# Side work placed by a list schedule at build time, seven products in another order, eight PSUM banks in rotation

## The chip, the core and the metric

One core of a Trainium2 chip runs the kernel in one launch. The metric is the device time of that launch in microseconds. A core has a matrix engine (PE, its weight loads shown apart as PEld), a vector engine (DVE), a scalar engine (ACT), a general engine (POOL) and an engine that issues most transfers (SP). Each takes its instructions strictly in the order in which the program wrote them; between engines, semaphores say when a result is there. Matmul results land in PSUM, which has eight banks; a bank can be written again only when its last reader is through.

## What is computed

A linear attention over 4 batches of 576 rows, a rank-32 mixing along the sequence, a dense two-layer block with 512 inputs and 2048 hidden features, and a mixture of 8 experts (512 to 1024 to 512) in which a gate chooses an expert for each row.

```python
u = x + h.transpose(0, 2, 1)                       # x: what attention gave, h: the rank-32 mixing
ch = np.maximum(u @ w_ch1, 0.0) @ w_ch2            # dense block, 2048 hidden
x = (u + ch)
...
for s in range(S):                                 # experts, batch by batch
    fresh_e = int(np.argmax(logits[b, s]))
    if s == 0 or local_gate[b, s] < 0.5:
        e = fresh_e
    else:
        e = prev_e if prev_e >= 0 else fresh_e
    ...
    h = np.maximum(x[b, s] @ w1[e], 0.0)
    out[b, s] = p[e] * (h @ w2[e])
```

## The kernel before

After the attention, all work is cut into 24 items. An item is one batch (576 columns, in two halves of 288) against one unit of 512 hidden features. Items 0 to 15 are the dense block: four units, each against four batches. Items 16 to 23 are the experts: for each batch the expert that most of its rows chose, in two units. (A loop at the end repairs the rows that chose another expert; it finds few or none.)

Numbers are float32, and a product of two is made of three matmuls on split values: each operand is kept as a high part in the matmul's type (`fp32r`) and the low remainder. So every operand needs an ACT cast (high part) and a subtraction on DVE or POOL (low part) before PE may use it. These casts and subtractions, the sums below, the conversion of the dense weights from 64-bit words (six DVE instructions and one POOL sum for each of eight pieces of a unit, `narrow`, L77 to L84) and the expert choice (`route`) are the side work.

The first layer of items 1 to 23 takes seven block products in place of eight (`seven_steps`), with sums of weight blocks (S1 to S4) and of input blocks (T1 to T4). A product is 12 matmuls of 288 columns. Results stay in PSUM in pairs of banks; DVE and ACT take them out, add them (`u2`, `u3`, `p1`, L799) and make the hidden features by `relu`: ACT writes `hhi` (L756), then DVE writes `hlo` (L757). Then come eight steps of the second layer (`mm2`, 12 matmuls each, L842 to L844), and DVE adds each result into `y` (L852). An item is so 84 + 96 = 180 matmuls in 15 steps; item 0 uses eight plain products (192 matmuls).

What sets the order: the program is written in one pass. After each step `side` moves three queues of generators on, `w` (next unit's weights), `x` (inputs of a coming item) and `r` (routing), a fixed number of yields each: one, or two in some items. Where a product needs an operand that isn't written yet, `need_w` or `need_x` runs its queue on until it is. PSUM for items comes from two pools, 3 banks and 2, chosen by a counter; three more banks belong to routing (`ps_r`). The routing of items 13 to 16 advances twice after every step, or once. `then(i)` names the inputs to be made for item i + 2. For i = 14 and for i = 15 that is the same key, expert input of batch 3, so these inputs are made twice.

Of the kernel before, what the change touches and what calls it, by code (L numbers as in the profile page):

```python
# [22 lines left out]
CH = 288  # L23
# [14 lines left out]
def model(ctx, tc, kq, vx, wphi, ident, up, vp, wff, wg, wmoe1, wmoe2, rconst, outT):  # L38
# [30 lines left out]
    def narrow(dst, raw, p, n, a=None):  # L69
# [7 lines left out]
        nc.vector.tensor_scalar(out=au, in0=hw, scalar1=0x7FFFFFFF, scalar2=None, op0=ALU.bitwise_and)  # L77
        nc.vector.tensor_scalar(out=b, in0=a, scalar1=F64_LO, scalar2=F64_MAX, op0=ALU.max, op1=ALU.min)
        nc.vector.tensor_scalar(out=au, in0=bu, scalar1=3, scalar2=0x3FFFFFFF, op0=ALU.logical_shift_left, op1=ALU.bitwise_and)
# [3 lines left out]
        nc.vector.tensor_scalar(out=bu, in0=au, scalar1=0xFF800000, scalar2=None, op0=ALU.bitwise_and)  # L83
        nc.vector.scalar_tensor_tensor(out=b, in0=lw, scalar=2.0 ** -52, in1=b, op0=ALU.mult, op1=ALU.mult)  # L84
        in_halves(nc.gpsimd, dst, a, b, n, ALU.add)
        rows.extend(own)
# [49 lines left out]
    tasks = {"w": [], "x": [], "r": []}  # L136

    def advance(kind):

        q = tasks[kind]  # L140
        if not q:
            return "none"
        said = next(q[0], "end")
        if said == "end":
            q.pop(0)
        return said

    def take(free):

        while not free:  # L150
            yield "blocked"
        return free.pop(0)
# [6 lines left out]
    def raw_dma():  # L159

        while order and rawfree:
# [7 lines left out]
            raws.append(t)  # L169

    def fetch():

        raw_dma()
        t = raws.pop(0)
        f = yield from take(rows)
        if wff.dtype == F32:
            nc.gpsimd.tensor_copy(out=f[:, :512], in_=t.bitcast(F32)[:, :512])
        else:
            yield from narrow(f[:, :512], t, 128, 512, f[:, :512])
        rawfree.append(t)  # L180
        raw_dma()
        return f
# [8 lines left out]
    def w_end(u, s, f, eng, back=None, apart=True):  # L191

        w = u.w[s] = yield from take(wfree)
        nc.scalar.copy(out=w[:, 0], in_=f[:, :512])  # L194
        if apart:
# [5 lines left out]
        yield  # L201

    def w_first():

        for s in BLOCKS + VS:
            f = yield from fetch()
            yield
            yield from w_end(units[0], s, f, nc.gpsimd, rows, False)

    def w_sums():  # L210
# [4 lines left out]
        def whole(name, eng):  # L215
            f = yield from take(rows)
            both(eng, f, f32(u.w[name][:, 0]), f32(u.w[name][:, 1]), ALU.add)
            return f
# [6 lines left out]
        yield  # L225
        both(p, s3, a11, a21, ALU.subtract)
        yield
        both(v, a21, a21, a22, ALU.add)
        both(v, a11, a21, a11, ALU.subtract)
        rows.append(a22)  # L230
        yield
        yield from w_end(u, "S2", a11, v)
        yield from w_end(u, "S1", a21, p, rows)
        a12 = yield from whole("A12", v)
        both(v, a12, a12, a11, ALU.subtract)
        rows.append(a11)
        yield
        yield from w_end(u, "S3", s3, p, rows)
        yield from w_end(u, "S4", a12, p, rows)

    def w_seven(u, get, free, eng, p):
# [4 lines left out]
        both(p, s3, a11, a21, ALU.subtract)  # L246
        yield
        yield from w_end(u, "S3", s3, eng, rows)
        a22 = yield from get("A22")
        both(p, a21, a21, a22, ALU.add)  # L250
        yield
        yield from w_end(u, "A22", a22, eng, free)
        yield from w_end(u, "A11", a11, eng)
        both(p, a11, a21, a11, ALU.subtract)
        yield
        yield from w_end(u, "S1", a21, eng, free)
        a12 = yield from get("A12")
        yield from w_end(u, "A12", a12, eng)
        both(p, a12, a12, a11, ALU.subtract)
        yield  # L260
        yield from w_end(u, "S2", a11, eng, free)
        yield from w_end(u, "S4", a12, eng, free)

    def w_ffn(u):

        def get(name):
            f = yield from fetch()
            yield
            return f

        yield from w_seven(u, get, rows, nc.gpsimd, nc.gpsimd)
        for s in VS:
            f = yield from get(s)
            yield from w_end(u, s, f, nc.gpsimd, rows)

    halfraw = []

    def w_moe(u):

        if not halfraw:  # L280
# [6 lines left out]
        ahead_ = []  # L287

        def load():
            while halfraw and todo_:  # L290
# [6 lines left out]
                else:  # L297
                    nc.sync.dma_start(out=t, in_=wmoe2[e, 4 * u.g + int(name[1])].rearrange("o p f -> (o p) f"))
                ahead_.append(t)
# [8 lines left out]
        load()  # L308
        yield
        yield  # L310
        yield from w_seven(u, get, halfraw, nc.vector, nc.gpsimd)
        load()
        yield
        for s in VS:
            f = yield from get(s)
            yield from w_end(u, s, f, nc.vector, halfraw)

    def need_w(u, s):
        while s not in u.done:
            said = advance("w")  # L320
            assert said not in ("none", "blocked"), (u.kind, u.b, u.g, s, said)
# [3 lines left out]
    XS = ("B11", "T2", "B21", "T1", "T3", "T4", "B22")  # L325
    xo, xdone, xd = {}, set(), {}

    def x_end(key, s, r, eng):

        x = xo[key][s] = yield from take(xfree)  # L330
        nc.scalar.copy(out=x[:, 0], in_=r)  # L331
        yield
        for k in range(2):
            eng.tensor_tensor(out=x[:, 1, k], in0=r[:, k], in1=f32(x[:, 0, k]), op=ALU.subtract)  # L334
        xdone.add((key, s))
        yield
# [4 lines left out]
    def x_make(key, keep=True, plain=False, adds=nc.gpsimd, lows=nc.gpsimd):  # L341
# [7 lines left out]
        def add(a, c):  # L349
            r = yield from take(rows)  # L350
            x = as_x(r)
            for k in range(2):
                adds.tensor_tensor(out=x[:, k], in0=a[:, k], in1=c[:, k], op=ALU.subtract)  # L353
            yield
# [6 lines left out]
        def own(s):  # L361
            yield from x_end(key, s, part[s], lows)
            save(s, part[s])

        def made(s, r):
            if not plain:
                yield from x_end(key, s, as_x(r), lows)
            save(s, as_x(r))

        if plain:  # L370
            for s in ("B11", "B21", "B12", "B22"):
                yield from x_end(key, s, part[s], lows)
                if s != "B12":
                    save(s, part[s])
# [3 lines left out]
        t2 = yield from add(part["B22"], as_x(t1))  # L378
        yield from made("T2", t2)
        t4 = yield from add(as_x(t2), part["B21"])  # L380
        rows.append(t2)
        if not plain:
            yield from own("B21")
        yield from made("T1", t1)
        rows.append(t1)
        t3 = yield from add(part["B22"], part["B12"])
        yield from made("T3", t3)
        rows.append(t3)
        yield from made("T4", t4)
        rows.append(t4)  # L390
        if not plain:
            yield from own("B22")

    def x_load(key):

        xo[key] = {}
        got_ = []

        def load(m):
            r = yield from take(rows)  # L400
            nc.sync.dma_start(out=r, in_=xd[key][m])
            got_.append(r)

        for m in range(2):
            yield from load(m)
            yield
        for m, s in enumerate(XS):
            r = got_.pop(0)
            yield from x_end(key, s, as_x(r), nc.gpsimd)
            rows.append(r)  # L410
            if m + 2 < len(XS):
                yield from load(m + 2)

    def need_x(key, s):
        while (key, s) not in xdone:
            said = advance("x")
            assert said not in ("none", "blocked"), (key, s, said)
# [224 lines left out]
    def attn_step(S_):  # L642
# [41 lines left out]
        if S_ == 11:  # L684
            tasks["x"].append(x_make(("f", 0), plain=True))
        if S_ == 17:
            tasks["x"].append(x_make(("f", 1)))
# [25 lines left out]
    def fps():  # L713
        nps[0] += 1
        pool = late["psg"] if late and nps[0] % 5 < 2 else ps_f
# [23 lines left out]
    def then(i):  # L739

        if i < 3:
            return x_make(("f", 3), adds=nc.vector) if i == 1 else None
# [5 lines left out]
    def h_tiles(i, t, f):  # L748
# [3 lines left out]
        return hhi, hlo  # L752

    def relu(i, t, f, src):
        hhi, hlo = h_tiles(i, t, f)
        nc.scalar.activation(out=hhi, in_=src, func=ACTF.Relu)  # L756
        nc.vector.scalar_tensor_tensor(out=hlo, in0=src, scalar=0.0, in1=f32(hhi), op0=ALU.max, op1=ALU.subtract)  # L757

    def three(ps, w, x, j, first, stop):

        for k in range(2):
# [3 lines left out]
            nc.tensor.matmul(ps, lhsT=w[:, 1, c], rhs=x[:, 0, k], start=False, stop=(stop and k == 1), skip_group_check=True)  # L765

    def plain_steps(i):
# [3 lines left out]
        for t in range(2):  # L771
            for f in range(4):
                ps = fps()[:, :CH]
# [461 lines left out]
```

## Time and profile before

| | us |
|---|---|
| median of 3 runs | 918.18 (916.46 to 920.95) |
| the profiled execution | 914.94 |
| its span (first to last instruction) | 913.1 |
| PE busy | 810.7 (89%) |
| DVE busy | 650.9 (71%) |
| ACT busy | 351.8 (39%) |
| POOL busy | 422.6 (46%) |

The profiled execution is 1.84 us longer than its span. It has these stretches: attention, with item 0 in its last third (to about 200.9 us), items 1 to 12 (to 557.8), items 13 to 16 with the routing (to 703.8), items 17 to 22 (to 884), and item 23 with the end. Matmul durations overlap, since they are pipelined, so the distance from one start to the next tells the rate.

### The profile page before, as it was taken

To read this page: it belongs to the slowest core of one execution; us is meant where nothing else is said; L and a number is where in the kernel's file an instruction comes from. 1 tells how busy PE (TensorE), PEld (TensorE's weight loads), DVE (VectorE), ACT (ScalarE), POOL (GpSimd) and SP (SyncE) were. 2 spreads that over 40 slices of the span, in tenths; PEclk is the share of its full clock that TensorE was granted. 3 is DMA by queue.
4 is the path that set the end of the run, shared out by engine and by line. 5 is a ranking of instruction groups with operands and counts; after the bars stand their busy time and mean duration, and the time that the engine had idled before them with its cause. 6 is when DMAs were issued, how large, how long until landed. Compare 5 with 4: busy or idle time off the path is not lost. (4 is left out here: it accounts for less than half of the span.)

```text
span 913.1 us, 20785 instructions
## 1 busy us (share of the span) xinstructions
PE 810.7 (89%) x8368; PEld 768.6 (84%) x8368; DVE 650.9 (71%) x1300; ACT 351.8 (39%) x801; POOL 422.6 (46%) x522
## 2 busy tenths in 40 slices
PE   8999999997698879997899899879788879888897
PEld 6899988997697879987799798868688778887897
DVE  7899997458668865479654775688957866767654
ACT  5677776533221232121232231215224435345341
POOL 1123672147844595045870443536332764735712
PEclk9999999998899899999899899989899999998999
DMA  5443654012301341014320213032032143232411
GB/s 172 139 155 126 200 169 155 2 40 88 111 24 61 118 150 41 1 47 132 114 76 1 86 52 117 30 99 87 14 123 83 31 133 93 80 114 58 145 55 53
DMA packets 43618, 81.60 MB, mean 89 GB/s; under 512 B 4800, under 2 KB 21312, under 8 KB 43520
## 3 DMA queue, kind: packets, MB, share of 16 engines
q1 hardware_dynamic: 39808, 76.65, 26.6%
q10 hardware_dynamic: 3456, 3.46, 1.1%
q8 instruction: 66, 1.08, 0.5%
q14 instruction: 32, 0.26, 0.1%
q0 software_dynamic: 256, 0.15, 0.1%
HBM read 62.40 MB, written 17.84 MB: 88 GB/s over the span
## 5 line engine op out<-in xcount | busy, mean ns | idle before, releaser
L763 PE MATMUL psf<-x,w 128*128 128x288 f32 x676 | 214.2, 317 | 61.8 <-DVE hlo L757 30.4
L842 PE MATMUL psf<-hhi,w 128*128 128x288 f32 x768 | 235.9, 307 | 16.8 <-DVE u L799 10.5
L844 PE MATMUL psf<-hlo,w 128*128 128x288 f32 x768 | 233.5, 304 | 1.6 <-DVE hlo L757 1.3
L843 PE MATMUL psf<-hhi,w 128*128 128x288 f32 x768 | 231.6, 302 | 0.0
L764 PE MATMUL psf<-x,w 128*128 128x288 f32 x676 | 209.0, 309 | 0.0
L765 PE MATMUL psf<-x,w 128*128 128x288 f32 x676 | 208.2, 308 | 0.0
L763 PEld LDWEIGHTS psf<-x,w 128*128 128x128 f32 x676 | 135.8, 201 | 72.7 <-DVE hlo L757 33.4
L842 PEld LDWEIGHTS psf<-hhi,w 128*128 128x128 f32 x768 | 149.4, 194 | 23.0 <-DVE u L799 12.4
L334 POOL TENSOR_TENSOR x<-row,x 128x288 fp32r<-128x288 f32 x148 | 129.5, 901 | 80.0 <-ACT x L331 61.6
L844 PEld LDWEIGHTS psf<-hlo,w 128*128 128x128 f32 x768 | 149.4, 195 | 6.7 <-DVE hlo L757 6.3
L843 PEld LDWEIGHTS psf<-hhi,w 128*128 128x128 f32 x768 | 149.4, 195 | 0.0
L765 PEld LDWEIGHTS psf<-x,w 128*128 128x128 f32 x676 | 136.4, 202 | 0.2 <-DVE w L189 0.2
L764 PEld LDWEIGHTS psf<-x,w 128*128 128x128 f32 x676 | 136.1, 201 | 0.0
L67 POOL TENSOR_TENSOR row<-row,row 128x256 f32<-128x256 f32 x90 | 69.2, 790 | 98.4 <-DVE row L84 95.4
L67 POOL TENSOR_TENSOR w<-row,w 128x256 fp32r<-128x256 f32 x88 | 72.6, 848 | 79.7 <-ACT w L194 78.3
L852 DVE TENSOR_TENSOR y<-psf,y 128x288 f32<-128x288 f32 x160 | 69.1, 450 | 54.7 <-PE psf L844 54.3
L194 ACT CAST w<-row 128x512 fp32r<-128x512 f32 x53 | 32.7, 620 | 163.0 <-POOL row L67 154.5
L756 ACT ACTIVATE hhi<-u 128x288 fp32r<-128x288 f32 x92 | 38.6, 442 | 130.6 <-DVE u L799 130.6
L189 DVE TENSOR_TENSOR w<-raw,w 128x512 fp32r<-128x512 f32 x80 | 61.8, 778 | 32.3 <-ACT w L194 31.5
L799 DVE TENSOR_TENSOR u<-psf,p 128x288 f32<-128x288 f32 x92 | 40.8, 453 | 55.9 <-PE psf L765 44.5
L757 DVE SCALAR_TENSOR_TENSOR hlo<-u,hhi 128x288 fp32r<-128x288 f32 x92 | 55.0, 618 | 29.4 <-ACT hhi L756 29.4
L334 POOL TENSOR_TENSOR x<-y,x 128x288 fp32r<-128x288 f32 x56 | 49.0, 896 | 54.5 <-ACT x L331 29.6
(125 smaller groups left out, 1274.4 us busy)
## 6 DMA issues: line engine op xcount, KB each, us to landing
raw<-in_wff SPq DMA_DIRECT2D x32, 512.0 KB, 3.5
raw<-in_wmoe SPq DMA_DIRECT2D x64, 256.0 KB, 2.8
row<-xd SPq DMA_DIRECT2D x42, 288.0 KB, 3.5
kq<-in_kq SPq DMA_DIRECT2D x14, 576.0 KB, 4.8
vt<-in_vx SPq DMA_DIRECT2D x16, 325.0 KB, 3.1
xd<-row SPq DMA_DIRECT2D x16, 288.0 KB, 3.6
ys<-y SPq DMA_DIRECT2D x4, 1152.0 KB, 5.6
xd<-y SPq DMA_DIRECT2D x12, 288.0 KB, 4.3
```

Of the source, the lines that this page charges most:

```text
L67: eng.tensor_tensor(out=dst[:, sl], in0=a[:, sl], in1=b[:, sl], op=op)
L189: eng.tensor_tensor(out=out, in0=a, in1=b, op=op)
L334: eng.tensor_tensor(out=x[:, 1, k], in0=r[:, k], in1=f32(x[:, 0, k]), op=ALU.subtract)
L757: nc.vector.scalar_tensor_tensor(out=hlo, in0=src, scalar=0.0, in1=f32(hhi), op0=ALU.max, op1=ALU.subtract)
L763: nc.tensor.matmul(ps, lhsT=w[:, 0, c], rhs=x[:, 0, k], start=(first and k == 0), stop=False, skip_group_check=True)
L764: nc.tensor.matmul(ps, lhsT=w[:, 0, c], rhs=x[:, 1, k], start=False, stop=False, skip_group_check=True)
L765: nc.tensor.matmul(ps, lhsT=w[:, 1, c], rhs=x[:, 0, k], start=False, stop=(stop and k == 1), skip_group_check=True)
L799: nc.vector.tensor_tensor(out=out, in0=a, in1=c, op=op)
L842: nc.tensor.matmul(ps, lhsT=wh, rhs=hhi, start=(f == 0), stop=False)
L843: nc.tensor.matmul(ps, lhsT=wl, rhs=hhi, start=False, stop=False)
L844: nc.tensor.matmul(ps, lhsT=wh, rhs=hlo, start=False, stop=(f == 3))
L852: nc.vector.tensor_tensor(out=dst, in0=ps, in1=dst, op=ALU.add)
```

## The change

Routines that yielded at fixed places now yield in front of each instruction, at a `gate`. The builder keeps a clock for each engine (`free`) and for each tile (`touched`), moved by a cost formula per instruction and by 0.1325 for each matmul. In the stage after attention, a side instruction is written only if its engine would be through with it by PE's clock plus an allowance from a table (`SLACK`, by engine and step of the item). `pump` offers the gate to all side routines after every step; a routine that is needed at once runs with the gate forced open (`until`).

The products' order is now A11, S2, S1, S3, A22, A12, S4 (before: A11, S2, A12, S1, S3, A22, S4), so that of the inputs is B11, T2, T1, T3, T4, B21, B22. `mm2` sums features in the order 2, 3, 0, 1. The last two `relu` of an item stand behind the first `mm2` step. The second PSUM pool has 5 banks, routing's own pool is gone, and items and routing take the eight banks in turn. Routing advances twice after each of the last eight steps of an item alone. From i = 15 on, `then` names the inputs of item i + 3. The copy of `y` for the repair loop goes out in four transfers of a quarter. The operations and the engines that do them are otherwise the same.

```diff
+    SYNC = 0.15
+    SLACK = {"DVE": (1.5, 0.4, 1.5, 0.1, -0.2, -0.2, -0.2, 1.0, 1.0, 1.0, 0.3, 2.0, 2.0, 2.0, 1.5),
...
+    def cost(eng, n):
+        return {"DVE": 0.075 + n / 960, "ACT": 0.17 + n / 1330, "POOL": 0.05 + n / 365}[eng]
...
+    def book(eng, dur, *keys):
+
+        at = max([free[eng]] + [touched.get(id(k), 0.0) for k in keys])
+        free[eng] = at + dur
+        for k in keys:
+            touched[id(k)] = free[eng] + SYNC
+        return free[eng]
+
+    def gate(eng, dur, *keys):
+
+        if not late:
+            yield "step"
+        while late and not force[0]:
+            at = max([free[eng]] + [touched.get(id(k), 0.0) for k in keys])
+            if at + (0.0 if eng == "POOL" else dur) <= free["PE"] + SLACK[eng][at_step[0]]:
+                break
+            yield "wait"
+        emitted[0] += 1
+        if late:
+            book(eng, dur, *keys)
...
-    XS = ("B11", "T2", "B21", "T1", "T3", "T4", "B22")
+    XS = ("B11", "T2", "T1", "T3", "T4", "B21", "B22")
...
-        pool = late["psg"] if late and nps[0] % 5 < 2 else ps_f
+        pool = late["psg"] if late and nps[0] % 8 < 5 else ps_f
...
-        if i + 2 < n and not held(i):
-            key = x_key(i + 2)
-            return x_make(key, keep=False, adds=nc.vector) if key[0] == "m" else x_load(key)
+        to = i + 2 if i < 15 else i + 3
+        if to < n and not held(i):
+            key = x_key(to)
+            return x_make(key, to, keep=False, adds=nc.vector) if key[0] == "m" else x_load(key, to)
...
-        product("A12", "B21", pa, False, True)
-        for j in range(2):
-            relu(i, 0, j, pa[j])
-        yield
-        product("S1", "T1", pe, True, True)
+        product("S1", "T1", "e", True)
...
+        product("A12", "B21", "a", False)
...
+        late["rest"] = lambda: [relu(1, j, u2[j], t2[j]) for j in range(2)]
...
-        for f in range(4):
+        for k, f in enumerate((2, 3, 0, 1)):
...
-            advance("r")
+        if step >= steps - 8:
+            for _ in range(2):
+                advance("r")
...
-        for _ in range(2 if u.kind == "moe" or i % 4 in (0, 3) else 1):
-            if advance("w") == "blocked":
-                break
-        for _ in range(2 if i < 3 or i > 14 else 1):
-            if advance("x") == "blocked":
-                break
+        pump()
...
-    late["psg"] = ctx.enter_context(tc.tile_pool(name="ps_g", bufs=2, space=PSUM))
-    late["psr"] = ctx.enter_context(tc.tile_pool(name="ps_r", bufs=1, space=PSUM))
+    late["psg"] = ctx.enter_context(tc.tile_pool(name="ps_g", bufs=5, space=PSUM))
```

What this does to the order, at two places. First DVE in item 8, the stretch from the second to the fifth product; `row<-raw` and `row<-row` are weight conversion, `u`, `p` and `hlo` take results out of PSUM. Before:

```order
L83 TENSOR_SCALAR row_85<-row_91 128x512
L84 SCALAR_TENSOR_TENSOR row_85<-raw_92,row_85 128x512
L77 TENSOR_SCALAR row_87<-raw_93 128x512
L78 TENSOR_SCALAR row_90<-row_87 128x512
L79 TENSOR_SCALAR row_87<-row_90 128x512
L757 SCALAR_TENSOR_TENSOR hlo<-psf,hhi 128x288 x2
L81 SCALAR_TENSOR_TENSOR row_87<-raw_93,row_87 128x512
L83 TENSOR_SCALAR row_90<-row_87 128x512
L84 SCALAR_TENSOR_TENSOR row_90<-raw_93,row_90 128x512
L799 TENSOR_TENSOR u_3647<-psf,p_3643 128x288
```

The same engine and stretch of the changed kernel (L885 is the add, L887 `hlo`):

```order
L90 SCALAR_TENSOR_TENSOR row_87<-raw_92,row_87 128x512
L77 TENSOR_SCALAR row_85<-raw_93 128x512
L885 TENSOR_TENSOR u_3644<-psf,p_3640 128x288
L885 TENSOR_TENSOR p_3640<-psf,u_3644 128x288
L885 TENSOR_TENSOR u_3645<-psf,p_3641 128x288
L885 TENSOR_TENSOR p_3641<-psf,u_3645 128x288
L885 TENSOR_TENSOR u_3644<-u_3644,psf 128x288
L887 SCALAR_TENSOR_TENSOR hlo<-u_3644,hhi 128x288
L885 TENSOR_TENSOR u_3645<-u_3645,psf 128x288
L887 SCALAR_TENSOR_TENSOR hlo<-u_3645,hhi 128x288
L887 SCALAR_TENSOR_TENSOR hlo<-psf,hhi 128x288 x2
```

Conversion instructions stood in front of `hlo` in blocks of three to five; now none stands between the fourth product's add and the last `hlo` of the seven products, and the rest of the conversion follows one or a few at a time between the `y` adds. Second, DVE in item 15, where the routing's second half runs (`trps` is PSUM with transposed gate values, `r_cnt` counts votes). Before, in the products' part:

```order
L940 COPY row_86<-trps 8x320
L943 SCALAR_TENSOR_TENSOR row_90<-row_87,row_90 8x576
L945 TENSOR_REDUCE r_cnt<-row_90 8x1
L946 TENSOR_TENSOR row_86<-row_86,row_90 8x576
L189 TENSOR_TENSOR w_97<-raw_93,w_97 128x512
L799 TENSOR_TENSOR u_3647<-psf,p_3643 128x288
L799 TENSOR_TENSOR p_3643<-psf,u_3647 128x288
```

In the changed kernel, in the `mm2` part of the same item:

```order
L885 TENSOR_TENSOR y<-psf,y 128x288
L1114 COPY row_85<-psf 8x256
L1114 COPY row_90<-psf 8x256
L1114 COPY row_84<-psf 8x256
L1114 COPY row_85<-psf 8x320
L1114 COPY row_90<-psf 8x320
L1114 COPY row_84<-psf 8x320
L1117 SCALAR_TENSOR_TENSOR row_85<-row_90,row_85 8x576
L1119 TENSOR_REDUCE r_cnt<-row_85 8x1
L1120 TENSOR_TENSOR row_84<-row_84,row_85 8x576
L469 TENSOR_TENSOR row_91<-y 128x288
L885 TENSOR_TENSOR y<-psf,y 128x288
```

The routing left the products' part of the item, and all of it now stands between the `y` adds of eight steps.

## Rows read from the trace of the kernel before

**Rows 1.** Waits of PE, whole run: line, releaser: us, times, longest.

```profile
PE psf L763 <- DVE hlo L757: 30.4, 13, 6.2
PE psf L763 <- ACT p L804: 11.5, 6, 4.7
PE psf L763 <- DVE u L799: 10.7, 7, 3.4
PE psf L842 <- DVE u L799: 10.5, 7, 2.3
PE trps L936 <- DVE tr L925: 9.5, 4, 3.1
PE psf L763 <- DVE y L852: 6.9, 7, 1.8
PE psf L842 <- ACT hhi L756: 6.0, 13, 0.6
...
PE psf L763 <- ACT w L194: 2.1, 3, 1.0
PE psf L844 <- DVE hlo L757: 1.3, 4, 0.4
```

**Rows 2.** Stretches: length, busy PE, PEld, DVE, ACT, POOL, clock, DMA.

```profile
200.90:557.80 356.90, 316.27 (x2162) 305.89 (x2161) 243.09 (x476) 94.59 (x205) 195.32 (x240) 0.93 0.23 73
557.80:703.80 146.00, 120.44 (x831) 112.65 (x830) 111.76 (x282) 43.08 (x94) 53.87 (x66) 0.92 0.25 81
703.80:884.00 180.20, 156.71 (x1082) 149.29 (x1082) 126.43 (x225) 80.20 (x172) 101.28 (x114) 0.97 0.32 94
```

**Rows 3.** Stretches again, of single items: 1, 6 and 15.

```profile
200.94:235.20 34.26, 28.78 (x183) 27.19 (x181) 31.44 (x58) 11.35 (x24) 24.24 (x28) 0.90 0.30 96
363.13:387.03 23.90, 23.90 (x182) 23.90 (x181) 10.99 (x26) 4.58 (x11) 1.57 (x2) 1.00 0.01 1
628.57:667.20 38.63, 30.48 (x210) 28.40 (x208) 33.61 (x80) 13.12 (x27) 21.37 (x26) 0.91 0.16 53
```

**Rows 4.** Timeline of DVE in item 8: start, length, line.

```profile
424.29 0.76 DVE L78 TENSOR_SCALAR row<-row 128x512 f32<-128x512 f32 x1
425.08 0.83 DVE L79 TENSOR_SCALAR row<-row 128x512 uint32<-128x512 uint32 x1
425.83 0.81 DVE L757 SCALAR_TENSOR_TENSOR hlo<-psf,hhi 128x288 fp32r<-128x288 f32 x2
```

**Rows 5.** Timeline of PE in item 8, the start after those rows.

```profile
426.33 0.40 PE L763 MATMUL psf<-x,w 128*128 128x288 f32 x1 [3.25 <-DVE hlo L757]
```

**Rows 6.** Timeline of PE, matmuls after a wait and later.

```profile
309.31 0.44 PE L765 MATMUL psf<-x,w 128*128 128x288 f32 x1
...
314.73 0.29 PE L765 MATMUL psf<-x,w 128*128 128x288 f32 x1
```

**Rows 7.** Groups by shape, DVE, items 1 to 12: dearest and cheapest conversion line.

```profile
L81 DVE SCALAR_TENSOR_TENSOR row<-raw,row 128x512 uint32<-128x512 uint32 x24 | 19.6, 815 | 0.3
...
L83 DVE TENSOR_SCALAR row<-row 128x512 uint32<-128x512 uint32 x24 | 12.0, 500 | 0.4
```

**Rows 8.** Groups by shape, DVE, items 13 to 16: sums of inputs.

```profile
L353 DVE TENSOR_TENSOR row<-y 128x288 f32<-128x288 f32 x8 | 4.4, 593 | 0.0
...
L353 DVE TENSOR_TENSOR row<-row,y 128x288 f32<-128x288 f32 x4 | 3.4, 879 | 0.0
...
L353 DVE TENSOR_TENSOR row<-y,row 128x288 f32<-128x288 f32 x4 | 1.6, 438 | 0.0
```

**Rows 9.** Groups by shape, DVE, `hlo` from `u`: items 1 to 12.

```profile
L757 DVE SCALAR_TENSOR_TENSOR hlo<-u,hhi 128x288 fp32r<-128x288 f32 x48 | 30.6, 657 | 18.1 <-ACT hhi L756 18.1
```

**Rows 10.** The same group in item 6 alone (364.5 to 386).

```profile
L757 DVE SCALAR_TENSOR_TENSOR hlo<-u,hhi 128x288 fp32r<-128x288 f32 x4 | 1.7, 456 | 1.0 <-ACT hhi L756 1.0
```

**Rows 11.** The same group in item 1 alone (201 to 235).

```profile
L757 DVE SCALAR_TENSOR_TENSOR hlo<-u,hhi 128x288 fp32r<-128x288 f32 x4 | 3.6, 908 | 2.1 <-ACT hhi L756 2.1
```

**Rows 12.** The page's costliest groups: low parts of weights on DVE.

```profile
L189 DVE TENSOR_TENSOR w<-raw,w 128x512 fp32r<-128x512 f32 x80 | 61.8, 778 | 32.3 <-ACT w L194 31.5
```

More of the change, by code (lines that the diff above doesn't have):

```diff
@@ L135, in model @@
     ereg = {}
-    tasks = {"w": [], "x": [], "r": []}
-    def advance(kind):
[L140 to L150, printed above, removed]
+    free = {"PE": 0.0, "DVE": 0.0, "ACT": 0.0, "POOL": 0.0}
+    touched = {}
+    threads = []
+    force = [False]
+    emitted = [0]
+    SYNC = 0.15
+    SLACK = {"DVE": (1.5, 0.4, 1.5, 0.1, -0.2, -0.2, -0.2, 1.0, 1.0, 1.0, 0.3, 2.0, 2.0, 2.0, 1.5),
+             "ACT": (0.3, 1.0, 1.0, 1.0, 0.5, 0.0, 0.5, 1.0, 1.0, 1.0, 1.0, 1.0, 1.0, 1.0, 1.0),
+             "POOL": (2.0,) * 15}
@@ L168, in raw_dma, with fetch @@
                 nc.sync.dma_start(out=t, in_=wff[u.g, i].bitcast(U32))
[L169 to L182, printed above, removed]
+            touched[id(t)] = max(free["PE"], touched.get(id(t), 0.0)) + 4.0
+            raws.append((u, name, t))
+    pieces = {}
+    def fetch(u):
+        for name in ("A21", "A11", "A22", "A12") + VS:
+            raw_dma()
+            while not raws or raws[0][:2] != (u, name) or len(rows) < 2 or len(rows) < 5 and not force[0]:
+                yield "blocked"
+                raw_dma()
+            t, f = raws.pop(0)[2], rows.pop(0)
+            if wff.dtype == F32:
+                yield from gate("POOL", cost("POOL", 512), t, f)
+                nc.gpsimd.tensor_copy(out=f[:, :512], in_=t.bitcast(F32)[:, :512])
+            else:
+                while not rows:
+                    yield "blocked"
+                parts = narrow(f[:, :512], t, 128, 512, f[:, :512], True)
+                for n_ in range(6):
+                    yield from gate("DVE", cost("DVE", 512), t, f)
+                    next(parts, None)
+                if late:
+                    book("POOL", cost("POOL", 512), f)
+            rawfree.append(t)
+            raw_dma()
+            pieces[u, name] = f
     def both(eng, out, a, b, op):
@@ L361, in own @@
         def own(s):
[L362 to L371, printed above, removed]
+            if late:
+                spawn("x", due, x_end(key, s, part[s], lows, None, lambda: save(s, part[s])))
+            else:
                 yield from x_end(key, s, part[s], lows)
@@ L374, in x_make, with made, then @@
                     save(s, part[s])
+        def made(s, r, last_=True):
+            def then():
+                save(s, as_x(r))
+                if keep:
+                    touched[id(r)] = max(free["PE"], touched.get(id(r), 0.0)) + 3.0
+                if last_:
+                    rows.append(r)
+            if plain:
+                then()
+            elif late:
+                spawn("x", due, x_end(key, s, as_x(r), lows, r, then))
+            else:
+                yield from x_end(key, s, as_x(r), lows)
+                then()
+        if plain:
+            for s in ("B11", "B21", "B12", "B22"):
+                yield from own(s)
         else:
```

434 lines of the change are left out of this document (274 added, 160 removed).

## The prediction

> **What bounds the kernel now.** I read the stretches first, because the stages differ. In items 1 to 12, 13 to 16 and 17 to 22 PE is the busiest engine, but it is neither always busy nor always at full clock: granted 0.93, 0.92 and 0.97 [rows 2]. Single items show what it can do. Item 6, which has almost no side work, takes 23.90 us with PE busy throughout and clock 1.00 [rows 3]: that is the floor of an item. Items 1 and 15 take 34.26 and 38.63 us, with DVE busy 31.44 and 33.61 [rows 3]. So side work comes in lumps, and DVE is the engine that is late in the lumps. On average it isn't the bound: over items 1 to 12 DVE is busy 243.1 us, and twelve floors are 12 x 23.90 = 286.8 [rows 2, 3].
>
> The list of PE's waits says what for [rows 1]. Four rows are L763, the first matmul of a product, released by whoever last read a bank (`hlo`, `p`, `u`, `y`): 30.4 + 11.5 + 10.7 + 6.9 = 59.5 us. These are waits for a free bank. Three rows are L842 and L844, second-layer matmuls that wait for hidden features: 10.5 + 6.0 + 1.3 = 17.8. The routing's transposes wait 9.5, weights 2.1. Together 88.9 us. One of them is seen whole in item 8: DVE does two conversion instructions of 0.76 and 0.83 us, then `hlo` twice, and PE starts the next product after 3.25 us without work [rows 4, 5].
>
> A second loss hangs on these. After a wait a matmul lasts 0.44 us, later 0.29 [rows 6]; the granted clock is then at the lower of its two levels, 1.2 in place of 2.4 GHz. What that costs is PE's busy time over the floor: 316.3 - 286.8 = 29.5 in items 1 to 12; 156.7 - 6 x 23.90 = 13.3 in items 17 to 22; in items 13 to 16, 120.4 us hold 831 matmuls, of which 831 - 4 x 180 = 111 or so are the routing's, at the stage's mean (120.4 / 831) 16.1 us, so 120.4 - 95.6 - 16.1 = 8.7 [rows 2, 3]. Sum 51.5. In all 140 of 914.9 us can be had at most.
>
> **The change part by part.**
>
> *Eight banks.* With five banks a new product waits for a reader a few steps back; an item takes 16 banks, so with eight a bank comes round after about eight steps, some 12 us at floor rate (23.90 x 8 / 15). None of the four L763 kinds reaches back so far, and the 59.5 us go. What is late next: the first `mm2` step takes the bank of A11 and A12, whose last reader is the `hlo` of A12, now the sixth product of seven. Only S4 (12 matmuls, 23.90 x 12 / 180 = 1.6 us) lies between. The nearest row for such a short chain is L842 waiting for `hhi`, 6.0 us in 13, 0.46 each [rows 1]. I charge 0.46 to each of 23 items: 10.6. Bounds: nothing, or all 59.5, if DVE is as late as now.
>
> *Products' order, features in the order 2, 3, 0, 1, last relu behind the first `mm2` step.* Each gives DVE a product or a step more before PE asks. Against the 17.8 us I take half, 8.9 left; bounds 0 and 17.8.
>
> *The list schedule.* It removes no conversion. Eight pieces of six instructions stand in each of three units, 144 instructions at 0.50 to 0.82 us, so 72 to 117 us of DVE in items 1 to 12 [rows 7]. What changes is their place: item 8 loses its blocks in front of `hlo`, and items that had none get some. By the order, weight-conversion instructions in items 2 to 11 are now about 6 to 18 an item; before it was 24 or none. At 18 x 0.82 + 11 = 26 us of DVE for the worst, against 31.4 in item 1 now, the fullest item is still a little over the floor, the others under it. This is the cover for the bank term: without it DVE stays late, and the half case below holds.
>
> *Routing.* The chain on DVE is the same, and PE's transposes still wait for it. It is now squeezed into eight steps of an item instead of fifteen, beside eight `y` adds. I charge the 9.5 us one and a half times, 14.3; bounds 0 and 19.
>
> *The second making of batch 3's inputs goes.* It takes eight of 16 sums on DVE, (4.4 + 3.4 + 1.6) / 2 = 4.7 us [rows 8], with seven casts and 14 subtractions on ACT and POOL. In items 13 to 16 DVE has 111.8 us of 146.0 [rows 2], so it is on the path for part of this at most. I count 0 beside the waits; bounds 0 and 4.7.
>
> *Queues.* Four transfers of `y` in place of one add SP instructions and no wait on the path; in-order neighbours are input loads for two items later. The gate's yields also cut the input making during attention finer, but PE is nearly always busy there. Both 0, bounds 2 either way.
>
> *Sum.* Waits left: 10.6 + 8.9 + 14.3 + 2.1 = 35.9 of 88.9, a gain of 53.0. The low clock follows the waits: 51.5 x 35.9 / 88.9 = 20.8 stay, gain 30.7. Together 83.7: 914.94 - 83.7 = 831.2. The median of the runs lies 918.18 - 914.94 = 3.2 over the profiled execution, so I say 835.
>
> **A rule against it.** `hlo` made from `u` takes 456 ns in item 6, where POOL is busy 1.57 of 23.90 us, and 908 ns in item 1, where POOL is busy 24.24 of 34.26; the mean over items 1 to 12 is 657 [rows 3, 9 to 11]. The builder's formula prices it at 0.075 + 288 / 960 = 0.375 us wherever it stands. The Trainium skill, page "SBUF — State Buffer", section "Who interferes with whom", says that a vector instruction with two SBUF inputs contends with a GpSimd instruction that reads SBUF, and that the one that comes second is held for the whole of the other. By that rule the change does harm that the sum leaves out, since POOL's work is spread over all items and no item is left undisturbed. The trace agrees as far as rows 10 and 11 go. What it would give is the second rival.
>
> **The rivals.**
>
> 1. *DVE stays late* (0.18). The formula undercharges DVE and charges routing nothing, so the bank waits turn into waits for `hlo` and `u`, and only half of them go. For it: 0.50 to 0.82 us measured against 512 / 960 + 0.075 = 0.61 [rows 7]. Against it: 243 of 287 us leave room. Left 29.8 + 17.8 + 14.3 + 2.1 = 64.0; gain 24.9 + 51.5 x 0.28 = 39.3; 914.94 - 39.3 + 3.2 = 879.
>
> 2. *POOL slows DVE in every item* (0.13). Six `hlo` an item read two SBUF tiles; at 908 in place of 657 ns [rows 9, 11] that is 12 x 6 x 0.25 = 18 us on DVE in items 1 to 12. If all of it reaches PE: 853.
>
> 3. *Near the floor* (0.17). Only the routing's 9.5 and the weights' 2.1 stay: gain 77.3 + 51.5 x 77.3 / 88.9 = 122.1, so 796.
>
> 4. *Slower: a side instruction blocks DVE's queue* (0.06). DVE waits 31.5 us in front of L189 for a cast that follows a POOL sum that follows a transfer [rows 12]; today most of that lies where DVE is idle anyway. If the builder's clock thinks the operand there and puts L189 in front of an add, everything behind it on DVE waits, then PE. With no bank wait saved: 31.5 x (1 + 51.5 / 88.9) = 49.7 more, 968. It decides the sign once such new waits exceed the 53.0 saved.
>
> That the change doesn't do what it says is excluded for the place of the work by the order of both kernels.
>
> **How the numbers follow.** The forecast of 835 has 0.46 (815 to 850). Rivals 1, 2 and 3 are faster too, except the tail of rival 1, whose bounds reach no change. A measurement of this kernel tells 0.5%, 4.6 us, from none. Faster: 0.46 + 0.13 + 0.17 + 0.15 = 0.91; within: 0.03; slower: 0.06. For 8 in 10 the range goes from the floor case to a little past the half case: 797 to 892.
>
> **What would show it.** L763 rows released by `hlo`, `p`, `u` and `y` should fall from 59.5 to some 10 us, and what stays should stand at the first `mm2` step (L1009) or at S3, which adds into banks that the `u2` adds must have read. The transposes should keep 10 to 20 us. Items 2 to 12 should take 24 to 27 us each, all alike, clock 0.97 or more. The stretch of items 13 to 16 should stay the slowest, some 33 us an item. If DVE's idle time in front of L189 grows while adds are queued, rival 4 is at work; if `hlo` from `u` takes 0.8 us or more in every item, rival 2; if second-layer waits grow past 20 us, rival 1.

## The result, and the profile after

The changed kernel takes 824.76 us (median of 4 runs, 823.74 to 830.81), the kernel before 917.32 in the same comparison. The ratio is 0.8997, 95% interval 0.8954 to 0.9041: faster, by some 92 us where 83 were forecast, and 10 us under the predicted 835. The profiled execution is the slowest of the four: 830.81 us, span 829.0. The forecast for it was 831.2.

The three stretches of the profile after, items 1 to 12, 13 to 16 and 17 to 22 (length, busy time of each engine, granted clock, share of DMA, GB/s), answer to [rows 2]:

```profile
197.47:509.89 312.42, 297.36 (x2163) 293.34 (x2162) 256.51 (x474) 94.61 (x205) 206.72 (x240) 0.98 0.26 85
509.89:640.92 131.03, 112.69 (x831) 106.62 (x830) 105.55 (x275) 40.51 (x90) 52.55 (x66) 0.96 0.24 80
640.92:799.91 158.99, 150.01 (x1083) 149.07 (x1082) 121.20 (x223) 76.72 (x167) 90.26 (x100) 0.96 0.36 109
```

They are 44.5, 15.0 and 21.2 us shorter; the attention in front ends 3.4 us earlier. DVE's busy time in the first stretch has not fallen, it has grown by 13 us: the work is the same and only stands elsewhere.

Single items of after, 2, 9, 12 and 15, beside [rows 3]:

```profile
225.43:255.99 30.56, 26.95 (x183) 26.71 (x182) 28.06 (x50) 7.04 (x16) 23.39 (x27) 0.89 0.32 96
408.17:437.91 29.74, 26.18 (x182) 25.53 (x181) 25.56 (x40) 10.09 (x21) 24.21 (x31) 0.94 0.33 106
485.98:509.89 23.91, 23.91 (x183) 23.91 (x182) 12.07 (x26) 7.86 (x17) 11.38 (x14) 1.00 0.07 27
572.29:609.70 37.41, 30.15 (x209) 28.58 (x208) 34.34 (x91) 11.79 (x25) 15.14 (x18) 0.91 0.22 75
```

Item 12 is at the floor, as are items 7, 8, 11, 19 and 21. Items 2 and 9 are not, and item 15, with its routing, hardly moved.

What PE waits for in after, the whole run (us, times, longest), answers to [rows 1]:

```profile
PE psf L912 <- DVE u L885: 20.9, 9, 4.3
PE psf L1130 <- DVE r_cnt L1119: 8.3, 4, 2.5
PE psf L1110 <- DVE tr L1099: 5.6, 4, 2.5
PE psf L1011 <- DVE hlo L887: 4.1, 4, 3.1
PE psf L1009 <- ACT hhi L901: 2.0, 5, 0.4
PE psf L914 <- DVE w L279: 1.4, 1, 1.4
```

Together 42.3 us, of 88.9 before. The first row is one place: the nine matmuls that open S3, the fourth product, which adds into a bank that DVE must first have read to make `u`. One of them, in item 18, on DVE and PE (start, length, line, idle time before and its releaser):

```profile
672.96 0.99 DVE L279 TENSOR_TENSOR w<-raw,w 128x512 fp32r<-128x512 f32 x1 [1.56 <-ACT w L285]
673.87 0.81 DVE L885 TENSOR_TENSOR u<-psf,p 128x288 f32<-128x288 f32 x2
...
674.37 0.61 PE L912 MATMUL psf<-x,w 128*128 128x288 f32 x1 [4.33 <-DVE u L885]
```

DVE waits 1.56 us in a side instruction for a cast, with the two `u` adds behind it, and PE waits for those: rival 4's mechanism. It stands so in items 18, 20 and 22, 9.0 of the 20.9 us. In items 1, 2, 3, 5 and 15, 10.4 us, DVE runs side work without a pause right up to the two adds, which is what rival 1 described.

### The profile page after: what moved, and what is told of

Same layout as the page of the kernel before. It is cut to its first block, busy times and chain, and to the rows that moved or that the text cites. A ratio compares the mean times of both kernels' runs of the same rounds, so it can differ in the third digit from the quotient of the medians.

```text
span 829.0 us, 20784 instructions
## 1 busy us (share of the span) xinstructions
PE 776.8 (94%) x8368; PEld 749.7 (90%) x8368; DVE 653.4 (79%) x1292; ACT 345.8 (42%) x794; POOL 422.1 (51%) x508
## 5 line engine op out<-in xcount | busy, mean ns | idle before, releaser
L1009 PE MATMUL psf<-hhi,w 128*128 128x288 f32 x768 | 231.5, 301 | 2.0 <-ACT hhi L901 2.0
L1011 PE MATMUL psf<-hlo,w 128*128 128x288 f32 x768 | 229.0, 298 | 4.2 <-DVE hlo L887 4.1
L1010 PE MATMUL psf<-hhi,w 128*128 128x288 f32 x768 | 228.7, 298 | 0.0
L912 PE MATMUL psf<-x,w 128*128 128x288 f32 x676 | 205.0, 303 | 20.9 <-DVE u L885 20.9
L914 PE MATMUL psf<-x,w 128*128 128x288 f32 x676 | 204.4, 302 | 1.4 <-DVE w L279 1.4
L913 PE MATMUL psf<-x,w 128*128 128x288 f32 x676 | 204.4, 302 | 0.0
L447 POOL TENSOR_TENSOR x<-row,x 128x288 fp32r<-128x288 f32 x140 | 124.6, 915 | 93.9 <-ACT x L444 70.7
L912 PEld LDWEIGHTS psf<-x,w 128*128 128x128 f32 x676 | 132.2, 196 | 23.0 <-DVE u L885 23.0
L1009 PEld LDWEIGHTS psf<-hhi,w 128*128 128x128 f32 x768 | 146.0, 190 | 5.2 <-ACT hhi L901 3.1
L1010 PEld LDWEIGHTS psf<-hhi,w 128*128 128x128 f32 x768 | 146.3, 191 | 0.0
L914 PEld LDWEIGHTS psf<-x,w 128*128 128x128 f32 x676 | 131.8, 195 | 1.6 <-DVE w L279 1.6
L913 PEld LDWEIGHTS psf<-x,w 128*128 128x128 f32 x676 | 132.1, 195 | 0.0
L885 DVE TENSOR_TENSOR y<-psf,y 128x288 f32<-128x288 f32 x160 | 71.0, 448 | 38.1 <-PE psf L1011 37.5
L279 DVE TENSOR_TENSOR w<-raw,w 128x512 fp32r<-128x512 f32 x80 | 65.7, 848 | 26.2 <-ACT w L285 19.0
L887 DVE SCALAR_TENSOR_TENSOR hlo<-u,hhi 128x288 fp32r<-128x288 f32 x92 | 58.2, 652 | 30.8 <-ACT hhi L901 30.8
L444 ACT CAST x<-row 128x576 fp32r<-128x576 f32 x70 | 45.5, 672 | 71.8 <-DMA row<-xd 34.7
L285 ACT CAST w<-raw 128x512 fp32r<-128x512 f32 x80 | 48.4, 621 | 54.8 <-POOL y L1029 33.1
L447 POOL TENSOR_TENSOR x<-y,x 128x288 fp32r<-128x288 f32 x50 | 45.3, 926 | 30.1 <-ACT x L444 23.1
```

The source lines that it names most:

```text
L279: eng.tensor_tensor(out=out, in0=a, in1=b, op=op)
L885: nc.vector.tensor_tensor(**kw)
L887: nc.vector.scalar_tensor_tensor(op1=op1, **kw)
L912: nc.tensor.matmul(ps, lhsT=w[:, 0, c], rhs=x[:, 0, k], start=(first and k == 0), stop=False, skip_group_check=True)
L913: nc.tensor.matmul(ps, lhsT=w[:, 0, c], rhs=x[:, 1, k], start=False, stop=False, skip_group_check=True)
L1009: nc.tensor.matmul(ps, lhsT=wh, rhs=hhi, start=(k == 0), stop=False)
```

## Experiments

Twelve kernels ran. Ratios are to the kernel before; a per cent is 9.2 us.

**The banks alone.** The kernel before with eight banks in turn, nothing else.

```diff
-        pool = late["psg"] if late and nps[0] % 5 < 2 else ps_f
+        pool = late["psg"] if late and nps[0] % 8 < 5 else ps_f
...
-            ps = ps_r.tile([72, 384], F32, tag="r1", bufs=2, name="trps")
+            ps = fps()[:72]
```

> The kernel before, with eight PSUM banks in rotation and nothing else (routing draws from the same eight). Theory of the prediction (a bank wait is DVE being late, so banks alone give about half): some 880 us, first-matmul waits on hlo, p, u and y from 59.5 to about 30 us, second-layer and add waits stay or grow. Rival 'banks alone do it': about 840 us, these waits under 12 us. Rival 'the placement alone does it': within 1% of 917 us.

Measured: 912.52, ratio 0.9954 [0.9936, 0.9973]. Four us, not thirty. PE's waits in this kernel:

```profile
PE psf L763 <- ACT p L804: 31.0, 9, 5.1
PE psf L763 <- DVE p L799: 22.5, 12, 3.2
PE psf L936 <- DVE tr L925: 12.5, 4, 4.2
PE psf L842 <- ACT hhi L756: 9.3, 13, 2.2
PE psf L763 <- DVE u L799: 4.7, 2, 3.4
PE psf L844 <- DVE hlo L757: 4.7, 13, 1.0
PE psf L763 <- DVE hlo L757: 4.2, 1, 4.2
```

L763 still waits 62.4 us (59.5 before). All nine waits for ACT's `p` stand at the start of A12, which adds into A11's banks and so needs their copy `p`; the twelve for DVE's `p` stand at S4, which adds into S1's. No number of banks removes these: they are reads of the sum so far. Why the copy is late is seen in item 5, on ACT, PE and DVE:

```profile
333.91 0.62 ACT L194 CAST w<-row 128x512 fp32r<-128x512 f32 x1 [10.43 <-POOL row L67]
334.44 1.24 ACT L331 CAST x<-row 128x576 fp32r<-128x576 f32 x2
335.58 0.69 ACT L804 COPY p<-psf 128x288 f32<-128x288 f32 x2
...
336.03 0.61 PE L763 MATMUL psf<-x,w 128*128 128x288 f32 x1 [5.14 <-ACT p L804]
...
336.00 0.82 DVE L799 TENSOR_TENSOR u<-psf,p 128x288 f32<-128x288 f32 x2 [5.88 <-ACT p L804]
```

ACT stood 10.43 us in a weight cast whose operand POOL had not made, with the copy behind it. DVE waited 5.88 us for the same copy. In each of the nine places the copy stands behind such a cast, or (items 18, 20, 22) behind casts and outputs that wait for POOL. So this third of PE's waits is a block at the head of ACT's queue. What lies behind the block differs: in items 5 and 9 POOL was busy for all 10.43 us of the cast's wait, in items 18, 20 and 22 it is POOL too, while in items 2, 4, 8 and 12 POOL waited in turn for DVE's conversions, and DVE was busy for nearly all of it (4.43 of 4.50 us in item 4).

**Banks and order, without the schedule.** The same with the new order of products and features, the last `relu` behind the first `mm2` step, and routing in the last eight steps; still fixed counts of yields.

```diff
-        for f in range(4):
+        for k_, f in enumerate((2, 3, 0, 1)):
...
+        if step >= steps - 8:
+            advance("r")
+            advance("r")
```

> Eight banks and the new order of products and features, last relu behind the first second-layer step, routing in the last eight steps; side work still by fixed counts, inputs of batch 3 still made twice. Theory: 5 to 15 us under the banks-only run, by fewer second-layer waits (17.8 us before). Rival 'the order costs nothing and gives nothing': the same as banks only within 4 us. Rival 'the order is most of it': under 850 us.

Measured: 905.92, 0.9896 [0.9867, 0.9925]. The waits go on to the next reader: second-layer matmuls wait 29.5 us for `hhi` in 29 places, S3 16.9 for `u`. Without the schedule, the order and routing's new place are worth 0.6% (from 0.9954 to 0.9896).

**The schedule, with the old order and five banks.** The changed kernel with products, features, `relu` and pools put back. The inputs of batch 3 are made once and routing stands in the last eight steps, as in the changed kernel.

```diff
-    XS = ("B11", "T2", "T1", "T3", "T4", "B21", "B22")
+    XS = ("B11", "T2", "B21", "T1", "T3", "T4", "B22")
...
-        pool = late["psg"] if late and nps[0] % 8 < 5 else ps_f
+        pool = late["psg"] if late and nps[0] % 5 < 2 else ps_f
```

> The list schedule with the old product order, the old feature order and the old five banks (three for routing). Theory: placement keeps the blocks away from the adds, but a bank still comes back after five steps: some 875 us. Rival 'the placement alone does it': 835 us or less. Rival 'banks alone do it': 900 us or more.

Measured: 852.2, 0.9291 [0.9247, 0.9334]. That is 65 us, between the theory's 875 and the rival's 835. The schedule carries most of it, but not alone: the single making, 7 us by itself (below), and routing's new place are in this kernel. Items 1 to 12, where neither plays a part, take 327.26 us in place of 356.90; items 13 to 16 133.66 (146.00) and 17 to 22 164.84 (180.20).

**The schedule, old order, eight banks.** As the last, with the pools of the changed kernel.

```diff
-        for k, f in enumerate((2, 3, 0, 1)):
+        for k, f in enumerate((0, 1, 2, 3)):
...
+        product("A12", "B21", "a", False)
+        yield
```

> The list schedule with eight banks, but the old order of products and of features and the last relu ahead of the second layer. Theory: about 835 us, 8 to 12 us over the changed kernel, with second-layer waits for hlo and hhi back at 12 to 18 us. Rival 'the order matters little': within 4 us of the changed kernel's 825. Rival 'the order is most of it': over 860 us.

Measured: 848.4, 0.9259 [0.923, 0.9289]. The banks add 0.3%, less than the two intervals resolve: PE's waits for `hlo` at the first matmul of a product, 22.8 us with five banks, are gone, but waits for weights and for `r_cnt` have come up in their place. The rest of the way to 0.8997, some 24 us, belongs to the order and what goes with it. Items 1 to 12 take 314.25 us here against 312.42 in after, so it is not earned there; items 13 to 16 take 137.39 (131.03) and 17 to 22 167.65 (158.99). The second layer waits 2.8 us for `hhi` and 7.3 for `hlo`, together 10.1, not 12 to 18. What the schedule changed for ACT's queue is seen in its waits; the first row is of the banks alone, the second of this kernel:

```profile
ACT w L194 <- POOL row L67: 152.8, 29, 10.4
```

```profile
ACT w L285 <- POOL row L67: 37.2, 17, 6.5
```

The schedule writes a cast only when its own clock says that POOL is through, and the copies stand behind such a cast less often. The two rows that led PE's waits with the banks alone, 31.0 and 22.5 us, are in this kernel:

```profile
PE psf L915 <- DVE p L888: 4.0, 3, 2.0
PE psf L915 <- ACT p L969: 3.9, 3, 2.7
```

**One making of batch 3's inputs.** The kernel before with this edit alone.

```diff
-        if i + 2 < n and not held(i):
-            key = x_key(i + 2)
+        to = i + 2 if i < 15 else i + 3
+        if to < n and not held(i):
+            key = x_key(to)
```

> The kernel before, with batch 3's expert inputs made once and the later ones named for item i + 3, nothing else. Theory: the second making is beside the waits, so 0 to 6 us under 917. Rival 'freeing seven input tiles and DVE's 4.7 us is a good part of what the list schedule run gave': 15 us or more under 917, in items 15 to 22.

Measured: 909.99, 0.9919 [0.9894, 0.9944]. That is 5 to 10 us, over the bound of 4.7 in the prediction. The gain stands where the prediction did not look. Item 21 before, and in this kernel:

```profile
824.32:856.17 31.85, 28.20 (x182) 27.15 (x181) 23.06 (x39) 12.48 (x26) 23.39 (x26) 0.89 0.20 56
```

```profile
828.51:853.21 24.70, 24.63 (x182) 24.02 (x181) 16.48 (x34) 9.32 (x20) 11.37 (x14) 1.00 0.31 93
```

Items 14 and 15 hold 16 of the sums on DVE in both kernels, since the next batch's inputs now take the place of the second making. Every later making moves one place ahead, and the last one, in item 21, goes. The other stretches of this execution are 4.9 us longer together, 1.6 at most in one item.

**Prices nearer to the measured ones.** The changed kernel with all three engines dearer in the builder's formula.

```diff
-        return {"DVE": 0.075 + n / 960, "ACT": 0.17 + n / 1330, "POOL": 0.05 + n / 365}[eng]
+        return {"DVE": 0.1 + n / 750, "ACT": 0.2 + n / 1220, "POOL": 0.05 + n / 325}[eng]
```

> The changed kernel with the builder's prices set near what the trace shows (DVE 0.1 + n/750, ACT 0.2 + n/1220, POOL 0.05 + n/325), the allowances as they are. Theory (DVE is undercharged, and a side instruction too many stands ahead of the u2 adds): the first-matmul waits on u fall from 20.9 to under 10 us, 815 us. Rival (the allowances already hold the undercharge; higher prices push weights and inputs to their last moment): 825 to 850 us, with waits for w or x in place of u.

Measured: 842.43, 0.9191 [0.9169, 0.9213], slower than after by 18 us. Both sides are seen in its trace. S3 waits 7.5 us in place of 20.9, and ten of the items 1 to 12 are within 1 us of the floor. But less side work fits in, weights come too late, and PE then waits for them:

```profile
PE psf L1010 <- DVE w L279: 10.9, 5, 2.9
PE psf L1009 <- ACT w L285: 9.9, 1, 9.9
...
PE psf L1010 <- POOL w L67: 6.5, 2, 5.6
```

Item 4 alone takes 44.26 us. A truer price helps only where the remaining steps still have room.

**The features' order.** The changed kernel with features 0, 1, 2, 3.

```diff
-        for k, f in enumerate((2, 3, 0, 1)):
+        for k, f in enumerate((0, 1, 2, 3)):
```

> The changed kernel with the second layer summing features in the order 0, 1, 2, 3. Features 0 and 1 come from A12, now the sixth product, so PE asks for them first. Theory: 3 to 8 us slower than the changed kernel by waits at the first second-layer matmul in most items. Rival 'eight products' time covers it': the same within 2 us. If most of the 24 us between old and new order sits here: 845 us.

Measured: 832.09, 0.9066 [0.9041, 0.9091]: 0.7% slower than after by the ratios, though the two intervals just meet. The wait of the second layer for `hhi` is 11.7 us in place of 2.0.

**The `u2` adds guarded.** The changed kernel, with no DVE side work let in late in the first two steps of an item.

```diff
-    SLACK = {"DVE": (1.5, 0.4, 1.5, 0.1, -0.2, -0.2, -0.2, 1.0, 1.0, 1.0, 0.3, 2.0, 2.0, 2.0, 1.5),
+    SLACK = {"DVE": (-0.4, -0.4, 1.5, 0.1, -0.2, -0.2, -0.2, 1.0, 1.0, 1.0, 0.3, 2.0, 2.0, 2.0, 1.5),
```

> The changed kernel with DVE's allowance after the first two products at -0.4 in place of 1.5 and 0.4, so that less side work stands ahead of the two u2 adds that the fourth product's banks wait for. Theory: the waits of the fourth product on u fall from 20.9 to under 8 us, 810 to 817 us. Rival (the work is only pushed on, and DVE lacks the time): waits appear at weights or in the second layer, 822 us or more.

Measured: 822.88, 0.8989 [0.8963, 0.9014], which can't be told from after. S3's waits fall from 20.9 to 15.0 us, not to under 8; items 18 and 20 still take 29.43 and 29.03.

**Routing spaced.** The changed kernel, with one yield more in front of routing's large transposes and two in front of the small matmul.

```diff
+        yield
         own = []
...
-        for _ in range(3):
+        for _ in range(5):
             yield
         ps = fps()[:1, :8]
```

> The changed kernel with one more yield before the routing's big transposes and two more before its small one, so that PE comes to them later. Theory (PE stands 13.9 us in items 13 to 16 because it reaches a transpose before DVE is through, not because DVE lacks time): these waits fall to under 7 us and the run is 6 to 12 us faster, 813 to 819. Rival (DVE is full there): the waits move to the fourth product or to the next item, 823 us or more.

Measured: 832.97, 0.9071 [0.9032, 0.911], slower than after by 8 us. Half of the theory held: the waits at the transposes fell from 13.9 to 5.6 us, as the 8.3 us for `r_cnt` went. But the run is slower, as the rival had it: S3 waits 24.6 us for `u` and 3.1 for `y`, and routing now runs on into the next item: item 16 takes 35.19 us (31.22 in after) and item 17 28.81 (24.21). Two instructions on DVE, in items 15 and 16, are long beside POOL's work, 4.49 and 3.70 us, and PE stands 3.06 and 3.29 us behind them. More on these below.

**Dearer prices in items 5 to 12 only.**

```diff
+        if not 5 <= at_item[0] <= 12:
+            return {"DVE": 0.075 + n / 960, "ACT": 0.17 + n / 1330, "POOL": 0.05 + n / 365}[eng]
+        return {"DVE": 0.1 + n / 750, "ACT": 0.2 + n / 1220, "POOL": 0.05 + n / 325}[eng]
```

> The changed kernel with the measured prices in items 5 to 12 alone. In the run with these prices everywhere, items 5 to 12 stood at 23.9 to 24.6 us each, and item 4 lost 20 us to late weights. Theory (the undercharge makes the waits of items 5 to 9, and only the early items lack the time for honest prices): items 5 to 12 fall from 203 to 194 us or less, 814 to 817 us in all. Rival (items 5 to 12 were quick there only because item 4 had stood for 20 us and let DVE and POOL get ahead): the waits stay or come back as waits for weights, 822 us or more.

Measured: 820.6, 0.8954 [0.8921, 0.8986]. It is the fastest median of the study, 4 us under after, though the intervals meet. Items 5 to 12 in its profile, and in after's:

```profile
307.66:500.57 192.91, 191.51 (x1442) 191.28 (x1441) 144.66 (x294) 59.14 (x130) 122.58 (x148) 1.00 0.26 83
```

```profile
306.95:509.89 202.94, 196.08 (x1443) 194.58 (x1442) 155.51 (x295) 58.95 (x130) 125.01 (x148) 0.98 0.25 78
```

Items 5 to 12 fell as the theory said, the whole time did not reach its 814 to 817. Items 6 to 12 are all at 23.91 us, the floor: 10 us between the two profiled executions, more than the medians show, and 5.8 of them in item 9 alone.

**Guard, spacing and prices together.** The three edits above in one kernel.

```diff
+    SLACK = {"DVE": (-0.4, -0.4, 1.5, 0.1, -0.2, -0.2, -0.2, 1.0, 1.0, 1.0, 0.3, 2.0, 2.0, 2.0, 1.5),
...
+        if not 5 <= at_item[0] <= 12:
```

> The guard of the u2 adds, the spaced routing and the measured prices in items 5 to 12 together. If the three gains add: 823 less 10 for the items 5 to 12 less 8 for the routing, 803 to 808 us. If they share one cause: no better than the best of them, 813 us or more.

Measured: 848.01, 0.9238 [0.9199, 0.9276]. They don't add. In item 8 (47.55 us) the second layer waits for weights that aren't made:

```profile
PE psf L1013 <- POOL w L67: 15.4, 1, 15.4
PE psf L1012 <- ACT w L288: 5.7, 1, 5.7
```

That the guard and the prices together leave the weights too little room fits this, but no run has these two alone.

**One allowance for all steps.** The changed kernel without its table.

```diff
-    SLACK = {"DVE": (1.5, 0.4, 1.5, 0.1, -0.2, -0.2, -0.2, 1.0, 1.0, 1.0, 0.3, 2.0, 2.0, 2.0, 1.5),
...
+    SLACK = {"DVE": (0.9,) * 15, "ACT": (0.9,) * 15, "POOL": (2.0,) * 15}
```

> The changed kernel with one allowance for every step of an item (DVE 0.9, ACT 0.9, about the tables' means; POOL 2.0 as it is); order of products and features, banks and schedule as in the changed kernel. It settles what the 24 us between list schedule with the old order (848.4) and the changed kernel (824.8) belong to, since that table was made for the new order. Theory 1, the order: PE has more work between a product and its reader whatever the table says, so the time stays at 822 to 832, and second-layer waits (mm2) stay under 10 us. Theory 2, the table: without small allowances in front of the steps that need DVE at once, side instructions stand in front of the features and weights again; second-layer waits and first products come back and the time goes to 838 to 855, as with the old order.

Measured: 835.02, 0.9088 [0.9062, 0.9113]. It falls between the two theories, and the second layer's waits, 11.6 us, do too. The table is worth 0.9% in the new order, so part of the 24 us may be a table that doesn't suit the old order; how much stays open.

## Why the prediction was right, and where it was not

**The size.** The sum was made against the profiled execution and gave 831.2; that execution took 830.81. The median lies 6 us lower, and the forecast had added 3.2. By rows: waits fell by 46.6 us (forecast 53.0). The low clock, taken as PE's busy time over the floor as in the prediction, is now 297.36 - 286.8 = 10.6, 150.01 - 143.4 = 6.6 and 112.69 - 95.6 - 111 x 112.69 / 831 = 2.0, together 19.2 (forecast 20.8), a gain of 32.3 against 30.7. These two make 78.9 of the 84.1 us between the profiled executions; the attention in front, put at 0, gave 3.4 more. That the sum came within 1 us is in part luck. The sign, the size of the clock's share and the routing were foreseen; the banks gave far less than their term, the order more, the second making 7 where 0 stood, and the schedule, which had no term of its own, most of all.

**Eight banks: the step that failed.** The prediction read the 59.5 us at L763 as waits for a free bank and let the bank rotation remove them. Part of that reading is wrong in the kernel before already: its 11.5 us behind ACT's `p` all stand at the start of A12, which adds into banks in use; the other 48.0 are waits for a free bank. The rotation alone removed 4 us, and the waits turned to the products that add into a bank: 62.4 us at L763, a little over the term's upper bound, "all 59.5, if DVE is as late as now". The list schedule was taken as a cover for this term, with half of it left if the cover failed. It is the carrier: 65 us with five banks, the single making and routing's place included. In the changed kernel 20.9 us are left at the first matmul of a product, twice the "some 10" that the prediction gave as a sign.

**What was late.** "DVE is the engine that is late in the lumps" was half the story. In item 8 DVE's conversions stand in front of `hlo` [rows 5]; but nine waits of the banks-alone kernel were ACT's queue, blocked at its head by a cast, with POOL's load behind five of them. ACT's waits in this form are the largest of its waits before, and are 61.2 us after:

```profile
ACT w L194 <- POOL row L67: 154.5, 30, 10.5
```

```profile
ACT w L285 <- POOL row L67: 61.2, 20, 5.7
```

This is the mechanism that rival 4 feared of the change [rows 12]. It was in the kernel before, on ACT, and the change took three fifths of these waits away. Much of ACT's idle time costs nothing; what it cost PE shows with eight banks and the old order, where PE's waits for the copy fall from 31.0 to 3.9 us once the schedule is in.

**The order: mis-sized.** It was put at 8.9 us of waits; with the schedule it goes with some 24, of which the features' order is 0.7% by itself and some part may be the table. The second-layer waits left, 2.0 + 4.1, are near the 8.9 forecast.

**Where the rest stands.** The main sum put 10.6 us at the first `mm2` step; there is almost nothing there. They are at S3, 20.9 us, the other place that the prediction named as a sign.

**Routing.** Forecast 14.3 us; measured 8.3 + 5.6 = 13.9. The stretch of items 13 to 16 stayed the slowest, 131.03 / 4 = 32.8 us an item (forecast 33).

**Second making.** Counted as 0 with 4.7 at most; alone it gave 7.4, interval 5 to 10. The place was wrong: the prediction took eight sums out of items 13 to 16, and the run shows them there still; what goes is the making in item 21, 31.85 us before and 24.70 with this edit. The bound also held DVE's instructions only, without the low clock that follows a wait, ACT and POOL. Its share beside the schedule was not measured; with the schedule and five banks item 21 takes 24.27 us.

**Rivals.** Rival 1 (builder undercharges, DVE stays late): S3's waits fall from 20.9 to 7.5 us with dearer prices, so the undercharge is there, and in five items DVE is late as this rival says; but those 13 us are far from the 44 that lie between this rival and the forecast. Rival 2 (POOL slows every `hlo`): not in that form. The group of [rows 9], in after:

```profile
L887 DVE SCALAR_TENSOR_TENSOR hlo<-u,hhi 128x288 fp32r<-128x288 f32 x48 | 32.0, 687 | 13.9 <-ACT hhi L901 13.9
```

One of the 48 took 6.17 us; the other 47 average (32.97 - 6.17) / 47 = 570 ns, less than the 657 before. Rival 3, the floor, holds in six items. Items 2 to 12 average 25.9 us, in the range of 24 to 27, but not "all alike": items 2 and 9 take 30.

## What to carry to other kernels

A wait for a PSUM bank can be a wait for the engine that reads it: before adding buffers, ask whether the next product would wait for the same reader. Then look on that reader's in-order queue for a side instruction that stands there without its operand; writing side work only when its operand should be ready was most of what gave 65 of the 92 us. Once such a schedule is tight, dearer prices or smaller allowances can come back as late weights elsewhere (18 us with dearer prices for all items, some 22 with the three edits together), so edits that look harmless alone are to be measured together.

## What was not expected of the hardware

An instruction of DVE can last to the end of an unbroken run of POOL instructions. In item 9 of after, DVE, POOL and then PE:

```profile
416.60 6.17 DVE L887 SCALAR_TENSOR_TENSOR hlo<-u,hhi 128x288 fp32r<-128x288 f32 x1 [0.51 <-ACT hhi L901]
...
416.65 3.09 POOL L447 TENSOR_TENSOR x<-row,x 128x288 fp32r<-128x288 f32 x4
419.70 1.40 POOL L67 TENSOR_TENSOR row<-row,row 128x256 f32<-128x256 f32 x2
421.07 1.40 POOL L67 TENSOR_TENSOR w<-row,w 128x256 fp32r<-128x256 f32 x2
...
422.83 0.40 PE L1011 MATMUL psf<-hlo,w 128*128 128x288 f32 x1 [3.12 <-DVE hlo L887]
```

The median of this instruction is 459 ns; here it ends 0.3 us after the last of eight POOL instructions that follow one another without a gap. The kernel with one allowance shows it twice, with 6.44 and 5.52 us; again the first ends just behind POOL's run:

```profile
317.09 6.44 DVE L885 SCALAR_TENSOR_TENSOR hlo<-u,hhi 128x288 fp32r<-128x288 f32 x1 [0.51 <-ACT hhi L899]
...
317.40 3.09 POOL L445 TENSOR_TENSOR x<-row,x 128x288 fp32r<-128x288 f32 x4
320.46 1.40 POOL L67 TENSOR_TENSOR row<-row,row 128x256 f32<-128x256 f32 x2
321.82 1.40 POOL L67 TENSOR_TENSOR w<-row,w 128x256 fp32r<-128x256 f32 x2
```

The same `hlo` is long in item 9 of all seven kernels that have the schedule and its first prices there, 3.73 to 6.49 us, and in item 5 of three of them, 5.54 to 6.44. All ten end 0.3 us behind POOL's run. With routing spaced, an instruction on 1x8 values took 3.70 us beside such a run (0.33 one item earlier), though it ended 0.7 us before the run did. The Trainium skill, page "SBUF — State Buffer", section "Who interferes with whom", lets the second comer wait for the whole of the other's instruction; that would be one POOL instruction of some 0.8 us, and the trace shows eight, so the measurement decides. In the kernel with dearer prices in items 5 to 12 no DVE instruction from item 1 on lasts over 1.8 us, and its item 9 takes 23.91 us in place of 29.74; in all three kernels with dearer prices there item 9 takes 23.91 us, in the seven others 29.0 to 31.4. That the hold is why is argued, not shown: no run took it away alone. And it is rare: of the 37 `hlo` from `u` in after that began while POOL worked, the other 36 took 0.46 to 1.10 us, two of them with over 20 us of POOL's run still to come. What decides between the two stays open.
